# First products on half the tokens, one x tile normalized on ScalarE first, q/k weights ahead of the second x block, one tile transposed by matmuls

## The chip, the cores and the metric

One core of a Trainium2 chip. The metric is device time in microseconds (us) of one execution, lower is better. "Span" is the time from the first to the last instruction of the profiled execution; it is about 1.7 us shorter than that execution's device time. The engines: PE is TensorE, DVE is VectorE, ACT is ScalarE, POOL is GpSimd, SP is the queue that issues the transfers (SPq).

## The reference, cut to what matters

```python
def reference(A_x, A_wqkv, A_wo, B_x, B_w1, B_w3, B_w2):     # x: 1 x 2048 x 1024, bf16
    xn = _layernorm(x, axis=-1)          # (x - mean) / sqrt(var + 1e-5), over the 1024 columns
    s = _A_ref(xn, A_wqkv, A_wo)         # q, k, v = xn @ wqkv (1024 x 3072); local dilated attention; @ wo
    g = _silu(_B_ref(xn, B_w1, B_w3, B_w2))   # silu(xn @ w1) * (xn @ w3), then @ w2; F = 3584
    ...                                  # s and g are combined by a recurrence along the tokens (cut)
```

Only the first 40 us of the program are touched by the change: layer norm of the first 512 tokens (x block one, four tiles of 128 tokens), their transposition, the first products with wqkv, and the preparation of the second 512 tokens (x block two). The products are done by Strassen's scheme on blocks; "eq" and "bq" are the first accumulators that need sums of weights and *differences of x blocks one and two*.

## The kernel before: the parts that matter

```python
def spin(ps, n):                       # n matmuls of zeros, to keep TensorE warm
    for k in range(n):
        nc.tensor.matmul(ps[:, k % 2], lhsT=warm[:, 0:P], rhs=warm[:], start=True, stop=True)

def ln_dve(c, sts):                    # layer norm of x tiles on VectorE (root on ScalarE)
    ...
        for h in range(2):
            nc.vector.bn_stats(out=stats[:, h, :], in_=xt4[:, st, h * 512:(h + 1) * 512])
        nc.vector.bn_aggr(out=mv[:, i, :], in_=stats[:])
    nc.scalar.activation(out=rstd[:], in_=mv[:, :, 1], func=ACTF.Sqrt, bias=eps_t[:], scale=1.0)
    nc.vector.reciprocal(out=rstd[:], in_=rstd[:])
    ...                                # tensor_scalar: (x - mean) * rstd

def ln_act(c, sts):                    # the same on ScalarE: Copy and Square with sums, Sqrt, Identity
    ...                                # two small steps (reciprocal, product) on VectorE

def ln_tp(c, st, dst, busy=0):         # transposes one x tile by eight matmuls with the identity
    tp = bank2(f"tp{c}_{st}")
    spin(tp, busy)
    ...

def xn_sums(b11, b21, b12, b22, o):    # four differences of x blocks one and two, VectorE
    nc.vector.tensor_sub(o[:, 0], b12, b11)      # "eq" needs this one
    nc.vector.tensor_sub(o[:, 1], b22, o[:, 0])  # "bq" needs this one
    nc.vector.tensor_sub(o[:, 2], b22, b12)
    nc.vector.tensor_sub(o[:, 3], b21, o[:, 1])

x_load(0)                              # four x tiles
wq0 = qkv_load(0, 0, slot(2, (4, D)))  # 1 MB each
x_load(1)
wq1 = qkv_load(0, 1, slot(6, (4, D)))
for st in range(NST):
    (ln_act if st == 2 else ln_dve)(0, [st])
...
tps = [ln_tp(0, st, [], busy=(5, 0, 1, 1)[st]) for st in range(NST)]
...                                    # eight copies out of PSUM: tiles 0, 1 VectorE, tiles 2, 3 ScalarE
wk0 = qkv_load(1, 0, slot(8, (4, D)))
wk1 = ...
qkv_load(2, 0, wve[0][:])
for st in range(NST):
    ln_dve(1, [st])
    ...                                # two DMA transposes of the tile of x block two
    if st == 1:
        qkv_load(2, 1, wve[1][:])
x_load(2)
...
for t, (w0, w1_, ws) in enumerate(...):          # q, k, v
    first_two(...)                     # products of width 512 with x block one
qkv_sums(wq0, wq1, sq)
xn_sums(xT[:, 0], xT[:, 1], b12, xT[:, 2], xs)
```

The Python order is not the order on an engine: a scheduler orders the instructions, each engine then takes its own list strictly in that order. `hp()` (high priority) and `issue_after` steer it.

## Time and profile before

| | before |
|---|---|
| device time, median of the first 3 runs | 726.93 us (725.63 to 726.95) |
| device time, 6 runs beside the changed kernel | 726.22 us (725.63 to 726.95) |
| span of the profiled execution | 725.4 us |
| TensorE busy | 715.2 us |
| first product / first full-width product with wq1 | 12.23 / 16.09 us |
| "eq" / "bq" | 34.05 / 35.78 us |

The four landmarks are starts in TensorE's timeline. Behind "bq" TensorE runs nearly without waits to the end, except for one stall near 675 us.

### The profile page before, as it was taken

What the parts mean: (1) busy time and instruction counts of PE and PEld (TensorE: products, weight loads), DVE (VectorE), ACT (ScalarE), POOL (GpSimd) and SP (SyncE); (2) the same over time, 40 slices, a digit from 0 to 9 for tenths busy, and PEclk for the clock granted to TensorE, in tenths of its full rate; (3) what the DMA queues carried; (4) which work ended last, traced back from release to release, by engine and by line L of the source; (5) the groups of instructions that cost most, each with busy time, mean ns of one, the idle gap of its engine ahead of it and who ended that gap; (6) DMA issues with size and microseconds to landing.
All of it is one profiled execution on the core that took longest, in us unless ns stands there. A gap on an engine that the chain in (4) does not pass through costs nothing.

```text
span 725.4 us, 8725 instructions
## 1 busy us (share of the span) xinstructions
PE 715.2 (99%) x3335; PEld 344.1 (47%) x3335; DVE 622.8 (86%) x678; ACT 313.9 (43%) x325; POOL 111.7 (15%) x171
## 2 busy tenths in 40 slices
PE   8999999999999999999999999999999999999996
PEld 4655656554444444444444444444444444444442
DVE  8795879779879878978999999969859989978984
ACT  5654434356555556554545312034364573020233
POOL 0011100011310300332212010000434006020011
PEclk9999999999999999999999999999999999999999
DMA  9966156877755453566756556469799445564515
GB/s 325 278 155 171 59 188 215 266 237 255 225 176 180 145 174 116 178 189 199 248 166 229 184 160 219 144 203 379 175 282 321 144 136 160 167 195 140 188 27 111
DMA packets 120137, 139.77 MB, mean 193 GB/s; under 512 B 18592, under 2 KB 95392, under 8 KB 119456
## 3 DMA queue, kind: packets, MB, share of 16 engines
q1 hardware_dynamic: 105552, 97.27, 44.1%
q0 software_dynamic: 14544, 41.95, 18.8%
q8 instruction: 26, 0.43, 0.2%
q14 instruction: 15, 0.12, 0.1%
HBM read 96.21 MB, written 38.80 MB: 186 GB/s over the span
## 4 chain that ended last, share of the span: by engine, by line
PE 92%; DVE 3%; ACT 2%; DMA 1%; issue 1%; SPq 0%; DVEq 0%; ACTq 0%
PE bm L149 20%; PE am L149 13%; PE em L149 13%; PE db L149 10%; PE bq L149 9%; PE de L149 7%; PE da L149 7%; PE eq L149 5%; PE aq L149 3%; PE wb L149 2%; PE we L149 2%; PE wa L149 2%; DVE stats L250 1%; DMA wve<-in_A_wqkv_dram 1%; PE af L149 1%
## 5 line engine op out<-in xcount | busy, mean ns | idle before, releaser
L149 PEld LDWEIGHTS <-wring 128*128 128x128 f16 (+1 forms) x1824 | 187.9, 103 | 207.5 <-issue 1.9
L149 PEld LDWEIGHTS <-h_sb 128*128 128x128 f16 (+1 forms) x1056 | 109.6, 104 | 119.4 <-issue 2.0
L149 PE MATMUL bm<-xs,wring 128*128 128x512 f16 x504 | 117.4, 379 | 0.1
L149 PE MATMUL am<-xT,wring 128*128 128x512 bf16 x336 | 79.7, 379 | 0.1
L149 PE MATMUL db<-wring,h_sb 128*128 128x512 f16 x336 | 73.2, 379 | 0.0
L474 DVE TENSOR_TENSOR BC<-Ep,vT 128x2048 bf16<-128x2048 bf16 x56 | 66.7, 1219 | 0.1
L419 DVE TENSOR_TENSOR pt<-qt,kT 128x4096 bf16<-128x4096 bf16 x24 | 55.0, 2290 | 0.7
L657 DVE TENSOR_TENSOR um<-em,um 128x1024 f32<-128x1024 f32 x28 | 34.2, 1223 | 20.9 <-PE em L149 20.0
L659 ACT ACTIVATE g<-um 128x1024 bf16<-128x1024 f32 x28 | 29.6, 1057 | 48.2 <-DVE um L657 48.2
L149 PE MATMUL da<-wring,h_sb 128*128 128x512 bf16 x224 | 49.0, 379 | 0.0
L460 POOL DMA_DIRECT2D Ep<-pb x64 | 37.9, 599 | 53.7 <-DVE pb L456 46.6
L149 PE MATMUL bm<-h_sb,wring 128*128 128x512 f16 x168 | 39.7, 379 | 0.0
L149 PE MATMUL em<-xs,wring 128*128 128x512 f16 x168 | 39.7, 379 | 0.0
L149 PE MATMUL em<-xT,wring 128*128 128x512 bf16 x168 | 39.7, 379 | 0.0
L484 DVE TENSOR_TENSOR oT<-oT,BC 128x2048 bf16<-128x2048 bf16 x32 | 39.0, 1220 | 0.4
L159 ACT COPY bm<-am 128x1024 f32<-128x1024 f32 x28 | 27.9, 998 | 26.0 <-PE am L149 26.0
L159 ACT COPY pm<-em 128x1024 f32<-128x1024 f32 x28 | 28.4, 1013 | 20.1 <-PE em L149 20.1
L159 ACT COPY um<-bm 128x1024 f32<-128x1024 f32 x28 | 28.4, 1013 | 19.2 <-PE bm L149 19.2
L678 ACT CAST g<-bm 128x1024 bf16<-128x1024 f32 x28 | 28.3, 1010 | 17.4 <-PE bm L149 17.4
L672 DVE TENSOR_TENSOR h_sb<-bm,pm 128x1024 bf16<-128x1024 f32 x21 | 25.6, 1218 | 5.1 <-PE bm L149 5.0
L421 DVE TENSOR_TENSOR pt<-pt 128x2048 bf16<-128x2048 bf16 x24 | 29.3, 1222 | 0.4
L962 POOL DMA_DIRECT2D out_dram<-h_sb x12 | 15.1, 1512 | 94.7 <-DVE h_sb L961 94.6
(197 smaller groups left out, 1019.5 us busy)
## 6 DMA issues: line engine op xcount, KB each, us to landing
wring<-in_B_w_dram SPq DMA_DIRECT2D x61, 512.0 KB, 4.5
wring<-t_dram SPq DMA_DIRECT2D x16, 512.0 KB, 3.7
t_dram<-wring POOLq DMA_DIRECT2D x14, 512.0 KB, 4.6
wring<-t_dram SPq DMA_DIRECT2D x16, 384.0 KB, 5.1
wring<-in_B_w_dram SPq DMA_DIRECT2D x12, 384.0 KB, 4.0
wring<-in_A_x_dram SPq DMA_DIRECT2D x16, 256.0 KB, 4.7
Ep<-pb POOLq DMA_DIRECT2D x64, 64.0 KB, 4.6
wring<-in_A_wo_dram SPq DMA_DIRECT2D x8, 512.0 KB, 5.7
```

What stands on the lines that cost most here:

```text
L149: anchor["pe"] = nc.tensor.matmul(ps, lhsT=lhs[k], rhs=rhs[k], start=(first and k == 0), stop=(k == n - 1), skip_group_check=not first,)
L159: nc.scalar.copy(out=out_, in_=in_)
L419: nc.vector.tensor_mul(p_t[:], q[:], kT[:, :, o:o + CH])
L421: nc.vector.tensor_add(p_t[:, 0:4, :], p_t[:, 0:4, :], p_t[:, 4:8, :])
L460: nc.gpsimd.dma_start(out=pr[c][r:P:NR, :, sq * P:(sq + 1) * P], in_=pb[sq * 32:(sq + 1) * 32, :, :])
L474: nc.vector.tensor_mul(dst, E[:, w, :].unsqueeze(1).to_broadcast([P, n, CH]), vT[:, js, o:o + CH])
L484: nc.vector.tensor_add(A, A, B if w0 else C)
L657: v = nc.vector.tensor_add(su2[:], pe[:], su2[:])
L659: nc.scalar.activation(out=hl["g"][:, :, CH:], in_=su2[:], func=ACTF.Silu)
L672: anchor["v"] = nc.vector.tensor_add(h[:, :, CH:], pb[:], sp5[:])
L678: nc.scalar.copy(out=hl["g"][:, :, 0:CH], in_=pb[:])
L962: nc.gpsimd.dma_start(out=rows_, in_=g, accum_op=ALU.add)
```

## The change

Its intent: let TensorE begin real products sooner (on the first 256 tokens while the others are still transposed), have the weights there in the order of their use, and take the transfer queue out of the way of the second path (transposes of x block two, then the differences).

```diff
+    wq1 = qkv_load(0, 1, slot(6, (4, D)))
+    wk0 = qkv_load(1, 0, slot(8, (4, D)))
     x_load(1)
-    wq1 = qkv_load(0, 1, slot(6, (4, D)))
-    for st in range(NST):
-        (ln_act if st == 2 else ln_dve)(0, [st])
...
-    tps = [ln_tp(0, st, [], busy=(5, 0, 1, 1)[st]) for st in range(NST)]
...                      # tpose(st, a): four transposes; untp(st, a, engine): copy out of PSUM
+    ln_dve(0, [0])
+    ln_act(0, [1])
+    ln_dve(0, [2])
+    ln_dve(0, [3])
+    def p1(g, th):       # 8 matmuls of 256 columns: token half th, weight group g
+        cols = slice(th * 2 * P, (th + 1) * 2 * P)
...
+        act_copy(snap[g][:, :, cols], pf[g][:, :, cols])
+    spin_in(0, 0, 5)
+    tpose(0, 0)
+    tpose(0, 1)
+    untp(0, 0, dve_copy)
+    untp(0, 1, sc_copy)
+    tpose(1, 0)
+    tpose(1, 1)
+    untp(1, 0, sc_copy)
+    untp(1, 1, sc_copy)
+    tpose(2, 0)
+    tpose(2, 1)
+    untp(2, 0, dve_copy)
+    p1(0, 0)
+    tpose(3, 0)
+    tpose(3, 1)
...
+    p1(1, 0)
+    p1(0, 1)
+    p1(1, 1)
...
-    TPE = ()
-    qkv_load(2, 0, wve[0][:])
+    TPE = (3,)           # tile 3 of x block two is transposed by matmuls
+    for h in I:
+        qkv_load(2, h, wve[h][:])
...
-        if st == 1:
-            qkv_load(2, 1, wve[1][:])
...
-                  *((lambda: None, 4) if t == 0 else (lambda: None, 0)))
-    tp1(*TPE)
-    qkv_sums(wq0, wq1, sq)
+                  *((lambda: None, [pf[0], pf[1]]), (lambda: None,), (lambda: tp1(*TPE),))[t])
+    with behind("x"):
+        qkv_sums(wq0, wq1, sq)
```

Cut: the bookkeeping of `first_two`, which takes over the products already begun, and a priority for the square roots of x blocks one and two. Six of the warming matmuls, between the transposes and ahead of the first product, are gone.

More of the change, by code (lines that the diff above doesn't have):

```diff
@@ L165, in flush, with first_two @@
             pend.pop(0)()
-    def first_two(key, A, b11, b21, snap, e11, mid=lambda: None, busy=0):
-        pa = []
+    def first_two(key, A, b11, b21, snap, e11, mid=lambda: None, pa=None):
+        have, pa = pa, pa or []
         for g in range(2):
-            pa.append(bank2(f"a{key}{g}"))
-            spin(pa[g], busy if g == 0 else 0)
-            for i in I:
-                mm(pa[g][:, i], A[g][0][i], b11, True)
-            act_copy(snap[g], pa[g][:])
+            if have is None:
+                pa.append(bank2(f"a{key}{g}"))
+                for i in I:
+                    mm(pa[g][:, i], A[g][0][i], b11, True)
+                act_copy(snap[g], pa[g][:])
         mid()
@@ L251, in ln_dve @@
             nc.vector.bn_aggr(out=mv[:, i, :], in_=stats[:])
-        nc.scalar.activation(out=rstd[:], in_=mv[:, :, 1], func=ACTF.Sqrt, bias=eps_t[:], scale=1.0)
-        nc.vector.reciprocal(out=rstd[:], in_=rstd[:])
+        with hp() if c < 2 else nullcontext():
+            nc.scalar.activation(out=rstd[:], in_=mv[:, :, 1], func=ACTF.Sqrt, bias=eps_t[:], scale=1.0)
+            nc.vector.reciprocal(out=rstd[:], in_=rstd[:])
         for i, st in enumerate(sts):
@@ L297, in xn_sums @@
         nc.vector.tensor_sub(o[:, 2], b22, b12)
-        nc.vector.tensor_sub(o[:, 3], b21, o[:, 1])
+        anchor["xs"] = nc.vector.tensor_sub(o[:, 3], b21, o[:, 1])
     def B_of(b11, b21, b22, o):
@@ L986 @@
     qt[0] = att_tile((NJ, CH), BF16, "qt0")
-    tps = [ln_tp(0, st, [], busy=(5, 0, 1, 1)[st]) for st in range(NST)]
-    for a in I:
-        for st in range(NST):
-            (nc.vector.tensor_copy if st < 2 else nc.scalar.copy)(
-                out=xT[:, a, :, st * P:(st + 1) * P], in_=tps[st][:, a].rearrange("p (k t) -> p k t", k=KH),
-            )
-    wk0 = qkv_load(1, 0, slot(8, (4, D)))
+    snap = [oT[:, i // 2, 4 * (i % 2):4 * (i % 2) + 4].rearrange("p j n -> p (j n)").bitcast(FP32).rearrange("p (i n) -> p i n", i=2) for i in range(4)]
@@ new lines, with tpose, untp @@
+    tpb = {}
+    def tpose(st, a):
+        key = a, st // 2
+        if key not in tpb:
+            tpb[key] = bank2(f"tp{a}{st // 2}")
+        tp = tpb[key]
+        for k in range(KH):
+            nc.tensor.matmul(
+                tp[:, st % 2, k * P:(k + 1) * P], lhsT=xt[0][:, st, (a * KH + k) * P:(a * KH + k + 1) * P], rhs=ident[:],
+                start=(k == 0), stop=(k == KH - 1), skip_group_check=True,
+            )
+    def untp(st, a, eng):
+        with hp():
+            r = eng(out=xT[:, a, :, st * P:(st + 1) * P], in_=tpb[a, st // 2][:, st % 2].rearrange("p (k t) -> p k t", k=KH))
+        if eng == dve_copy:
+            anchor["x"] = r
@@ new lines @@
+    dve_copy, sc_copy = nc.vector.tensor_copy, nc.scalar.copy
+    ln_dve(0, [0])
+    ln_act(0, [1])
+    ln_dve(0, [2])
+    ln_dve(0, [3])
+    pf = {}
+    def p1(g, th):
+        if g not in pf:
+            pf[g] = bank2(f"af0{g}")
+        cols = slice(th * 2 * P, (th + 1) * 2 * P)
+        w = wq0.rearrange("p k (c two j) -> p k two j c", two=2, j=4)
+        for i in I:
+            for k in range(KH):
+                nc.tensor.matmul(
+                    pf[g][:, i, cols], lhsT=w[:, k, 0, 2 * g + i, :], rhs=xT[:, 0, k, cols],
+                    start=(k == 0 and th == 0), stop=(k == KH - 1), skip_group_check=True,
+                )
+        act_copy(snap[g][:, :, cols], pf[g][:, :, cols])
@@ new lines, in spin_in @@
+    def spin_in(st, a, n):
+        tpb[a, st // 2] = bank2(f"tp{a}{st // 2}")
+        spin(tpb[a, st // 2], n)
+    spin_in(0, 0, 5)
[13 more added lines that the diff above has]
+    tpose(3, 1)
+    untp(3, 0, dve_copy)
+    untp(2, 1, sc_copy)
+    untp(3, 1, dve_copy)
+    p1(1, 0)
@@ L1012 @@
     sq = [sq[:, q] for q in range(3)]
-    snap = [oT[:, i // 2, 4 * (i % 2):4 * (i % 2) + 4].rearrange("p j n -> p (j n)").bitcast(FP32).rearrange("p (i n) -> p i n", i=2) for i in range(4)]
     Bq = B0, B_of(xT1[0], xT1[1], xT1[3], xs1)
```

## The prediction

> **What bounds the kernel now.** I read the page first, then TensorE's own waits, then TensorE's timeline over the first 40 us, then the same stretch of the transfer queue and of VectorE, because the diff touches nothing after it.
>
> ```profile
> PE 715.2 (99%) x3335; PEld 344.1 (47%) x3335; DVE 622.8 (86%) x678; ACT 313.9 (43%) x325; POOL 111.7 (15%) x171
> ```
>
> TensorE is busy in 715.2 us of a span of 725.4 us. Only TensorE's idle time, or work of TensorE that is not needed, can be removed. Its waits are few:
>
> ```profile
> PE warm L141 <- DVE warm L138: 1.3, 1, 1.3
> PE de L149 <- ACT dsp L159: 1.1, 1, 1.1
> PE af L149 <- DMA wve<-in_A_wqkv_dram: 0.4, 1, 0.4
> PE af L149 <- DMA wring<-in_A_wqkv_dram: 0.2, 1, 0.2
> ```
>
> Two of these are in the stretch that is changed (both "af"), and they are small. But "busy" hides the head: until 12.23 us TensorE runs zero matmuls that keep it warm, and transposes. In TensorE's timeline the columns are start, busy time, instruction and, in brackets, the idle time before it:
>
> ```profile
> 7.89 1.35 PE L281 MATMUL tp<-ident,wring 128*128 128x128 bf16 x16 [0.36 <-DVE wring L255]
> 9.07 0.59 PE L141 MATMUL tp<-warm 128*128 128x512 bf16 x2
> 9.96 1.07 PE L281 MATMUL tp<-ident,wring 128*128 128x128 bf16 x16 [0.29 <-ACT wring L275]
> 11.13 1.04 PE L141 MATMUL af<-warm 128*128 128x512 bf16 x4
> 12.23 3.61 PE L149 MATMUL af<-xT,wring 128*128 128x512 bf16 x16
> 16.09 7.12 PE L149 MATMUL af<-xT,wring 128*128 128x512 bf16 x32 [0.24 <-DMA wring<-in_A_wqkv_dram]
> ...
> 26.50 3.62 PE L149 MATMUL af<-xT,wve 128*128 128x512 bf16 x16
> 30.54 3.67 PE L149 MATMUL af<-xT,wve 128*128 128x512 bf16 x16 [0.42 <-DMA wve<-in_A_wqkv_dram]
> 34.05 1.89 PE L149 MATMUL eq<-xs,h_sb 128*128 128x512 f16 x8
> 35.78 1.89 PE L149 MATMUL bq<-xs,h_sb 128*128 128x512 f16 x8
> ```
>
> From 12.23 us on the products follow each other at 16 per 3.46 us (23.05 to 26.50), 0.216 us each. Against that pace the second half of the first product lost 0.4 us (12.23 + 3.46 = 15.69, it begins at 16.09: the second q weight block landed at 16.04), and the last v half lost 0.58 us (26.50 + 3.46 = 29.96, begins at 30.54: the second v block was issued at 24.01, behind four transposes, and landed at 30.49). The remaining length of the program is TensorE at its pace, so what the head saves should arrive at the end almost whole. Every later stretch where VectorE waits (102 us in total) ties it to TensorE again; the last such wait for TensorE before the one 1.1 us stall (at 676.96) is at 583.5, so that stall moves along too.
>
> The second path is the one to watch. "eq" needs the first difference of the second x block, "bq" the third one that is made:
>
> ```profile
> 29.25 1.26 SPq L1004 DMA_TRANSPOSE xT<-wring  x1
> ...
> 31.95 1.23 DVE L295 TENSOR_TENSOR xs<-h_sb,xT 128x2048 f16<-128x2048 bf16 x1 [3.97 <-DMA h_sb<-wring]
> 33.09 1.22 DVE L297 TENSOR_TENSOR xs<-xT,h_sb 128x2048 f16<-128x2048 bf16 x1
> 34.23 1.22 DVE L296 TENSOR_TENSOR xs<-xT,xs 128x2048 f16<-128x2048 bf16 x1
> ```
>
> VectorE stood idle 3.97 us for the transposes, and its third difference is done at 34.23 + 1.22 = 35.45, only 0.33 us ahead of "bq" at 35.78. TensorE can come forward by little before this chain (transposes by DMA, then three differences) holds it.
>
> **What the Trainium skill says.** "TensorE: Matmul & The Clock Gate", section "Wait — 56ns, not 53.3ns?", gives warm starts of 55.6 ns apart at 128 columns and 215.7 ns at 512; the trace has 216 ns. My estimate for 256 columns from its formula, N / 2.4 GHz + 2.5 ns, is 109 ns, so halving the tokens of a product costs nothing in array time. The same page, "What's actually happening", has the clock halve after an idle window of about 3.4 us. The trace's first matmuls are 0.43 us apart up to 5.97 us and 0.21 us afterwards; the change drops six warming matmuls, and the longest gap that I expect in the new head is 1.5 us, so I expect full speed.
> "DMA: Bandwidth & Descriptors", "Queues, rings and completion order", says that descriptors of one engine's ring are consumed in order. The trace agrees: transfers land in the order of issue, 1 MB in 2.71 us (wq0 at 10.62, the x block at 13.33, wq1 at 16.04, wk0 at 18.75, wk1 at 21.46). That is 387 GB/s, above the 358 GB/s that "Where 436 GB/s comes from" on that page calls the HBM limit; the measurement decides.
>
> **The change part by part.** The instruction orders of the two programs differ on TensorE in the first ~310 entries, on VectorE in the first 85, on ScalarE in the first 33, on the transfer queue in the first dozen; behind that they are the same.
>
> 1. *Tile 1 normalized on ScalarE first, instead of tile 2.* Tile 1 lands at 4.12, tile 2 at 4.89. Copy 4.14 to 5.20, Square 5.5 to 6.6, Sqrt 7.0; VectorE's two small steps reach it at 8.2, Identity (1.24) ends at 9.45. Before, it ended at 9.90. Tile 3 on VectorE slips to 10.6 (before 9.28), which matters less now.
> 2. *First products on half the tokens.* ScalarE then does the square root of tile 3 (0.3) and two copies of 0.51: 10.8. The first 8 matmuls of 256 columns begin near 10.85 (wq0 lands at 10.62), take 8 x 0.109 = 0.87, to 11.7; tile 3's transposes 0.45 to 12.2; the second group to 13.1; the other halves of both groups 1.75, to 14.85, with VectorE's copy of tile 3 (0.62 after 12.0) and ScalarE's snapshots just ahead of them. The full-width products with wq1 then begin at 14.85, not 16.09: **1.24 us gained**, if wq1 is there, and it now lands third, at 10.62 + 2.71 = 13.33.
> 3. *Weights ahead of x block two.* wk0 at 16.04, x tiles at 16.7 to 18.75, wk1 21.46 as before, v blocks 24.1 and 26.9 (no longer split by transposes). TensorE needs wk0 at 18.3, wk1 at 21.75, v at 25.2 and 29.2: no wait. **0.58 us gained** at the v block.
> 4. *One tile by matmuls:* 8 x 0.056 = **0.45 to 0.5 us added** on TensorE between the two v halves, and two ScalarE copies of 0.51; two of eight DMA transposes go (1.25 us of issue each).
>
> Sum on TensorE's own path: 1.24 + 0.58 - 0.5 = 1.3 us; "eq" at 32.7, "bq" at 34.45.
>
> The other path: VectorE now makes the q sums first (3 x 1.14, from 13.6 to 17.0), then the statistics of x block two; tile 0 is normalized near 20.8 (before 15.2), tiles 1 and 2 near 23.5 and 24.0. The transposes so begin 5.5 us later and queue behind the second v block (26.85). From the trace's pattern (the fourth was issued just as the block ahead landed, later ones every 1.25 us, landing 1.8 us after issue), the fifth lands near 30.4 and the sixth near 31.7. VectorE's k sums end near 30.4, ScalarE's copies of the tile by matmul near 31.0. Three differences from 30.5, the second waiting for the last transpose: 31.7, 32.9, 34.05. "bq" may begin at 34.1 against TensorE's 34.45. Both paths give the same gain within their error: **about 1.3 us**, 726.9 - 1.3 = 725.6.
>
> **The rivals.** (a) The transposes become the bound: if their issue takes 2.5 us each, as the first two of before did, the sixth lands near 33.8, the differences end near 36.1, and all is lost: 727. For it: they are later by 5.5 us and behind 2 MB more; against it: two fewer, nothing between them, and the long issues fell while the queue was full. (b) ScalarE's serial work (its statistics, four copies and four snapshots between 4 and 15 us) delays the halves, or wq0 lands after 10.9: gain under 0.5 us, 726.5. (c) The clock falls in the sparser head: up to 2 us of half speed, 727. (d) More is won: the copies overlap better and wq1's early arrival takes all the slack: 2 us, 724.9.
>
> **Range and chances.** The before runs alone spread from 725.63 to 726.95. I take 725.5, from 724.2 to 727.0. Two per cent are 14.5 us; before the first product there are only 12.2 us, so neither faster nor slower by over 2% is likely.
>
> **What would show it.** First product near 10.9 with 256 columns; full-width products from 14.9 without a wait for wq1; no wait for the v block; "bq" near 34.4. If a wait of TensorE for VectorE's differences stands at "eq" or "bq", rival (a) has happened. Matmuls of 256 columns 213 ns apart would show (c). The prediction is wrong if the gain at "bq" is not there at the end, or if it is above 2.5 us.

## More of the kernel before

The prediction shows TensorE's lines. What it does not show, and what became important, is VectorE's timeline of the kernel before (columns: start, busy time, instruction, count, and in brackets the idle time before it with what ended it):

```profile
3.52 1.88 DVE L250 BATCH_NORM_STATS2 stats<-wring 128x6 f32<-128x512 bf16 x3 [2.28 <-DMA wring<-in_A_x_dram]
...
5.43 1.23 DVE L250 BATCH_NORM_STATS2 stats<-wring 128x6 f32<-128x512 bf16 x2
6.58 0.14 DVE L253 RECIPROCAL rstd<-rstd 128x1 f32<-128x1 f32 x1
...
7.30 0.53 DVE L255 TENSOR_SCALAR wring<-wring,mv,rstd 128x1024 bf16<-128x1024 bf16 x1
```

Tile 0 landed at 3.50 and its statistics take two instructions, but its scaling stands at 7.30, behind the statistics of other tiles. If one of those lands late, tile 0 waits as well. In this profile none was late enough to show a wait.

## The result

| | before | after |
|---|---|---|
| device time, 6 runs each | 726.22 us (725.63 to 726.95) | 725.22 us (724.67 to 727.57) |
| ratio after / before | | 0.999 (95% interval 0.9975 to 1.0005) |
| span of the profiled execution | 725.4 | 723.5 |
| first product | 12.23 | 10.88 |
| first full-width product with wq1 | 16.09 | 14.83 |
| first product with wk1 (af<-xT,h_sb) | 23.05 | 21.74 |
| "eq" / "bq" | 34.05 / 35.78 | 32.64 / 34.37 |
| stall near 675 us | 1.09 | 0.56 |

Ratios are the mean time of one kernel's fast runs over that of the other's of the same rounds, so not quite the ratio of the medians quoted. The result is correct. 725.5 was predicted, 725.22 came out.

TensorE's timeline of the changed kernel, from its first product to "bq" (columns as before). The counts of the groups can be too small: some matmul records are missing from the trace (the page counts 3299 matmuls against 3353 weight loads), so starts are read here, not counts:

```profile
10.88 1.03 PE L1022 MATMUL af<-xT,wring 128*128 128x256 bf16 x8
...
12.20 2.79 PE L1022 MATMUL af<-xT,wring 128*128 128x256 bf16 x24
14.83 7.07 PE L149 MATMUL af<-xT,wring 128*128 128x512 bf16 x31
...
25.28 3.62 PE L149 MATMUL af<-xT,wve 128*128 128x512 bf16 x15
28.73 0.61 PE L282 MATMUL tp<-ident,wring 128*128 128x128 bf16 x8
29.18 3.62 PE L149 MATMUL af<-xT,wve 128*128 128x512 bf16 x16
32.64 1.89 PE L149 MATMUL eq<-xs,h_sb 128*128 128x512 f16 x8
34.37 1.89 PE L149 MATMUL bq<-xs,h_sb 128*128 128x512 f16 x8
```

No bracket stands behind any of these: from its first product up to "bq" TensorE waits for nothing. Half products follow at 24 in 2.63 us (12.20 to 14.83), 0.110 us each, half of the 0.216 us of a full one. The three largest waits of TensorE (engine and line, what it waited for, us in total, times, longest):

```profile
PE warm L141 <- DVE warm L138: 1.3, 1, 1.3
PE de L149 <- ACT dsp L159: 0.6, 1, 0.6
PE tp L997 <- DVE wring L256: 0.5, 1, 0.5
```

Both waits for weights are gone; the third line and two smaller ones lie ahead of the first product. The second path, VectorE's differences:

```profile
30.47 1.23 DVE L296 TENSOR_TENSOR xs<-h_sb,xT 128x2048 f16<-128x2048 bf16 x1 [0.32 <-ACT h_sb L288]
31.61 1.22 DVE L298 TENSOR_TENSOR xs<-xT,h_sb 128x2048 f16<-128x2048 bf16 x1
32.75 1.22 DVE L297 TENSOR_TENSOR xs<-xT,xs 128x2048 f16<-128x2048 bf16 x1
```

What "bq" needs is done at 32.75 + 1.22 = 33.97, 0.40 us ahead of "bq"; it was 0.33 us before. Its last wait is no more for a DMA (3.97 us before) but 0.32 us for ScalarE's copy of the tile that matmuls transposed.

"bq" is 1.41 us earlier, and the same 1.41 us stands at the landmarks behind it ("zp" 155.29 to 153.88 and 482.41 to 481.00). The span is 1.83 us shorter, since the stall near 675 us is also 0.53 us smaller (1.41 + 0.53 = 1.94; 0.1 us is lost elsewhere). So the trace says 1.4 us, the medians say 1.0 us, and the interval of the ratio includes zero. Two questions follow: does each part of the change do what its working says, and why do the runs of one kernel spread more (724.67 to 727.57) than the gain?

### The profile page after: what moved, and what is told of

The parts are those of the page before. It is cut to its first block, busy times and chain, and to the rows that moved or that the text cites. A ratio compares the mean times of both kernels' runs of the same rounds, so it can differ in the third digit from the quotient of the medians.

```text
span 723.5 us, 8711 instructions
## 1 busy us (share of the span) xinstructions
PE 711.4 (98%) x3299; PEld 345.8 (48%) x3353; DVE 623.2 (86%) x678; ACT 314.8 (44%) x329; POOL 111.9 (15%) x171
## 4 chain that ended last, share of the span: by engine, by line
PE 80%; DVE 7%; issue 6%; ACT 2%; DMA 2%; POOL 2%; DVEq 0%; ACTq 0%; POOLq 0%
PE bm L149 18%; PE am L149 13%; PE em L149 12%; PE bq L149 9%; PE eq L149 5%; PE db L149 5%; PE de L149 4%; PE da L149 3%; PE aq L149 3%; PE af L149 2%; PE wb L149 2%; DVE BC L475 2%; PE we L149 1%; PE wa L149 1%; POOL Ep L461 1%
## 5 line engine op out<-in xcount | busy, mean ns | idle before, releaser
L149 PEld LDWEIGHTS <-wring 128*128 128x128 f16 (+1 forms) x1808 | 185.7, 103 | 205.4 <-issue 1.6
```

The lines of the kernel that those rows point to most:

```text
L149: anchor["pe"] = nc.tensor.matmul(ps, lhsT=lhs[k], rhs=rhs[k], start=(first and k == 0), stop=(k == n - 1), skip_group_check=not first,)
```

## The experiments

**Theory.** The parts act as in the prediction's sum, TensorE's own path sets "bq", and the path of transposes and differences is 0.4 us behind it. **Rivals.** The head is set by something the sum takes as fixed (when x tiles land, in which order VectorE works); or the clock of TensorE falls in some executions; or the second path takes over as soon as a part is changed.

All twelve kernels give correct results. Profiles, landmarks in us from the span's start; "tile 2" is the landing of x tile 2 of block one, "full" the first full-width product with wq1:

| run | tile 2 | first | full | eq | bq | stall | span |
|---|---|---|---|---|---|---|---|
| before | 4.89 | 12.23 | 16.09 | 34.05 | 35.78 | 1.09 | 725.4 |
| after | 5.16 | 10.88 | 14.83 | 32.64 | 34.37 | 0.56 | 723.5 |
| e1 again | 5.84 | 11.57 | 15.52 | 33.34 | 35.06 | 0.26 | 723.9 |
| e2 full width | 5.78 | 12.76 | 16.25 | 34.31 | 36.67 | none | 725.5 |
| e3 all by DMA | 5.29 | 11.02 | 14.96 | 32.94 | 35.45 | 0.30 | 724.2 |
| e4 v split | 5.88 | 11.61 | 17.20 | 37.14 | 38.87 | none | 727.5 |
| e5 x first | 5.49 | 11.23 | 15.59 | 33.34 | 35.07 | 0.34 | 724.0 |
| e6 tile 2 on ScalarE | 5.46 | 11.49 | 15.44 | 33.25 | 34.98 | 0.56 | 724.2 |
| e7 steps on GpSimd | 5.63 | 11.78 | 16.72 | 34.44 | 36.17 | 0.90 | 725.7 |
| e8 e7 + order of differences | 6.01 | 11.81 | 15.55 | 33.27 | 35.00 | 0.58 | 724.2 |
| e9 warming matmuls | 5.83 | 11.78 | 15.66 | 33.52 | 35.25 | none | 723.8 |
| e10 order of VectorE | 5.29 | 11.32 | 15.32 | 33.04 | 34.77 | 0.87 | 724.3 |
| e11 several together | 5.86 | 10.90 | 17.85 | 35.88 | 37.60 | none | 726.1 |
| e12 before, again | 5.66 | 15.13 | 18.58 | 35.85 | 37.58 | 0.95 | 727.0 |

Span minus "bq" minus stall is 688.5 to 688.8 us in every row. So the profiled span is "bq", plus that constant, plus the stall: the stall is a second source of spread, and it does not follow "bq" (none at 35.25 and at 37.60, 1.09 at 35.78 and 0.95 at 37.58). The traces settle what sets it. In every profile GpSimd issues a load, vT<-v_dram, 613.2 us behind "bq" (613.5 in e2), VectorE waits for it, and the chain of VectorE's work that ends the stall starts there. VectorE's timeline of the kernel before:

```profile
654.66 1.22 DVE L474 TENSOR_TENSOR oT<-Ep,vT 128x2048 bf16<-128x2048 bf16 x1 [6.03 <-DMA vT<-v_dram]
```

The load lands 4.43 to 5.62 us after its issue, and in all ten profiles with a stall the stall is that time less 4.53 us, to 0.01 us (5.62 and 1.09 before, 5.08 and 0.56 after, 4.79 and 0.26 in e1). In the four without one it took 4.43 to 4.53. So the 0.53 us that the stall gave the changed kernel's profile are the chance of one transfer, not a gain of the change.

### e1: the changed kernel, unaltered

No edit.

> The changed kernel, unaltered, as a control. Main theory: the gain is made in the head of TensorE's timeline and only shifts the rest, so a second profile has the first product at 10.9 us, full-width products from 14.8, bq at 34.4, and in the timed rounds about 1.0 us (0.14%) less than before. The stall of TensorE near 675 us, which was 1.1 us in the profile of before and 0.6 us in that of after, is chance: anywhere from 0.4 to 1.2 here. Rival: that stall was shortened by the change and is 0.6 again.

725.67 us (725.15 to 726.09, 5 runs) against 726.15 for before; ratio 0.9994 (0.9981 to 1.0006). In its profile the head is 0.69 us later at every landmark. VectorE's timeline of this run:

```profile
5.87 0.69 DVE L250 BATCH_NORM_STATS2 stats<-wring 128x6 f32<-128x512 bf16 x1 [0.71 <-DMA wring<-in_A_x_dram]
6.48 0.15 DVE L254 RECIPROCAL rstd<-rstd 128x1 f32<-128x1 f32 x1
```

Tile 0's reciprocal stands behind the first statistics of tile 2, and these wait 0.71 us for tile 2, which landed at 5.84 instead of 5.16. First product minus landing of tile 2 is 5.72 (after), 5.73 (e1, e3, e4) and 5.74 (e5) in the five profiles with this head: the landing passes through one for one. The prediction's sum takes this landing as fixed. So the expectation failed: the landmarks came 0.7 us late, the gain was about 0.5 us by the medians and not 1.0, and the stall of 0.26 us lies below the 0.4 to 1.2 expected. That the stall is chance, and not an effect of the change as the rival has it, is borne out by the load described above.

### e2: halving undone

```diff
-        cols = slice(th * 2 * P, (th + 1) * 2 * P)
+        cols = slice(0, CH)
...                      # p1(0, 0) and p1(1, 0) only, after all the transposes
```

> Halving undone: the first products wait for all four tiles, everything else as in the changed kernel. Main theory: first product near 12.1 us (tile 3 normalized at 10.8, transposed to 11.3, copied by VectorE to 12.0), full-width second half 16 x 0.216 later at 15.55 instead of 14.83, no wait for a weight block, bq at 35.1, time 0.7 us longer than the changed kernel, so about 0.3 us under before. Rival (the halves are not what gains; the other path sets bq anyway): bq within 0.2 us of 34.4 and the same time.

727.21 us (726.87 to 728.20), ratio to before 1.0017; 1.54 us above e1's median of the same rounds. Against e1, whose tile 2 landed nearly alike: first product +1.19, full width +0.73, as expected; but "bq" +1.61, twice what was expected. VectorE's timeline shows the rest:

```profile
32.44 0.69 DVE L250 BATCH_NORM_STATS2 stats<-wring 128x6 f32<-128x512 bf16 x1 [2.68 <-DMA wring<-in_A_x_dram]
33.05 1.21 DVE L296 TENSOR_TENSOR xs<-h_sb,xT 128x2048 f16<-128x2048 bf16 x1
```

The scheduler put a statistics instruction of x block *three* ahead of the first difference, and VectorE stood 2.68 us until its data landed, though the first difference had its last input at 31.76; TensorE waited 0.19 us at "eq" and 0.44 us at "bq". So halving is worth 0.73 us at the full-width products, confirmed, and the other 0.9 us belong to an order that changed with the edit.

### e3: no tile by matmuls

```diff
-    TPE = (3,)
+    TPE = ()
```

> All four tiles of x block two transposed by DMA, as before; no matmul transposes there; everything else changed. Main theory: the two added transposes land near 31.6 and 32.9 us, so the three differences end near 35.2 and TensorE, which would be ready for bq at 33.9, begins it near 35.2: about 0.9 us lost against the changed kernel, with waits of TensorE for VectorE at eq and bq. Rival (the matmul transposes only cost TensorE 0.45 us and hide nothing): bq near 33.9 and a time 0.45 us shorter.

726.74 us (725.91 to 727.47), ratio 1.0008; 1.07 us above e1's median of the same rounds. TensorE's timeline:

```profile
32.94 1.92 PE L149 MATMUL eq<-xs,h_sb 128*128 128x512 f16 x8 [0.46 <-DVE xs L296]
35.45 1.89 PE L149 MATMUL bq<-xs,h_sb 128*128 128x512 f16 x8 [0.59 <-DVE xs L297]
```

The last two transposes landed at 31.46 and 32.75 (31.6 and 32.9 expected), and TensorE waits for the differences twice. In the changed kernel "bq" is 34.37 - 14.83 = 19.54 us behind the first full-width product, without a wait; counted from 14.96, "bq" would stand at 34.50 with the tile by matmuls, and at 34.06 without it if nothing waited (the tile takes 0.44 us, shown below). It stands at 35.45. So the tile costs 0.44 us of TensorE and saves 1.39 us of delay, 0.95 us net; 0.9 was expected. Here the second path sets "bq": the rival is real at a distance of one transposed tile.

### e4: the second v block behind four transposes, as before

```diff
-    for h in I:
-        qkv_load(2, h, wve[h][:])
+    qkv_load(2, 0, wve[0][:])
...
+        if st == 1:
+            qkv_load(2, 1, wve[1][:])
```

> The second v block issued behind the transposes of two tiles, as before; everything else changed. Main theory: it is issued near 26.4 us and lands near 29.9, TensorE needs it at 29.18 and waits 0.6 to 0.9 us; eq near 33.4, bq near 35.2; time 0.7 us longer than the changed kernel. Rival (the wait for the v block was covered by the differences in any case): bq within 0.2 us of 34.4 and the same time.

730.09 us (729.22 to 732.23), ratio 1.0065, the slowest of all. Two causes, in TensorE's timeline:

```profile
11.61 1.53 PE L1022 MATMUL af<-xT,wring 128*128 128x256 bf16 x8
...
33.63 3.67 PE L149 MATMUL af<-xT,wve 128*128 128x512 bf16 x16 [2.00 <-DMA wve<-in_A_wqkv_dram]
```

First, the v block was issued at 27.75 and landed at 33.58, 4.64 us after the fourth transpose (28.94). In the kernel before it landed 2.88 us after that transpose (27.61 and 30.49), and a block behind another block there took 2.64 to 2.71 us. TensorE waited 2.00 us, where 0.6 to 0.9 was expected. The block lost its time at its start: the core's transfers ran at 78 GB/s from 29 to 30 us, 207 from 30 to 31 and 410 from 31 to 32. In the kernel before it was issued 3.60 us ahead of the fourth transpose's landing, here 1.19 us; that this is the reason is not shown. Second, eight half products took 1.53 us instead of 1.03 in the same head: TensorE's clock fell. Between first and full-width product lie 5.59 us, not 3.95, so 1.64 us were lost. That has nothing to do with the edit, which comes 16 us later; all four timed runs of e4 have a mean granted clock of 0.993 to 0.996. Hence the rival of the falling clock, told below. With two causes mixed, the time of e4 is no measure of the v block's order; the wait of 2.00 us is, for this one execution.

### e5: x block two ahead of wq1 and wk0

```diff
+    x_load(1)
     wq1 = qkv_load(0, 1, slot(6, (4, D)))
     wk0 = qkv_load(1, 0, slot(8, (4, D)))
-    x_load(1)
```

> Order of loads undone: x block two ahead of the second q block and the first k block; everything else changed. Main theory: the second q block lands near 15.2 us instead of 12.5, TensorE, ready at 14.83, waits about 0.4 us; k and v blocks land in time; differences not later; bq near 34.8, time 0.4 us longer than the changed kernel. Rival (early x tiles matter more, because VectorE's statistics and the transposes start earlier): bq at or under 34.4 and the same or a shorter time.

726.12 us (725.42 to 727.41), ratio 0.9995. wq1 landed at 15.52; TensorE would have been ready at 11.23 + 3.95 = 15.18 and began at 15.59, 0.41 us late. That is the size expected, but the wait expected is not the one in the trace. TensorE's timeline:

```profile
13.79 1.97 PE L1022 MATMUL af<-xT,wring 128*128 128x256 bf16 x16 [0.20 <-DVE xT L1004]
```

The eight half products ahead of these began at 12.54, so at 0.110 us each the next were due at 13.42; they began at 13.79, 0.37 us late, because VectorE's copies of tile 3 came behind statistics of x block two, which had landed earlier in this order. The last of these sixteen began at 15.49 and the full-width product 0.11 us after it, so wq1, there since 15.52, cost nothing more. Alone it would have cost about 0.4 us: two delays lie over each other. The new order of loads is worth about 0.4 us here, but the run does not show which of the two it removes.

### e6: tile 2 on ScalarE instead of tile 1

```diff
-    ln_act(0, [1])
-    ln_dve(0, [2])
+    ln_dve(0, [1])
+    ln_act(0, [2])
```

> Tile 2 on ScalarE and tile 1 on VectorE, as before; everything else changed. Main theory: tile 1 is normalized by VectorE near 8.3 us, but its copies out of PSUM stay on ScalarE, which is busy with tile 2 until about 9.95, so the first product begins near 11.0 and the full-width products near 15.0; time 0.2 us longer than the changed kernel. Rival (tile 1 on ScalarE is what makes the early start): first product later than 11.5 and 0.6 us or more lost.

726.10 us (725.69 to 728.52), ratio 1.0003. TensorE waits 1.56 us for ScalarE's tile and begins its products at 11.49; with tile 1 on ScalarE and the same landing (5.46) it would be 5.46 + 5.73 = 11.19. The choice of the tile is worth 0.3 us.

### e7 and e8: tile 1's small steps on GpSimd; the order of the differences

```diff
...                      # mhalf: a constant tile of -0.5
-        nc.scalar.activation(out=v[:, 2], in_=v[:, 1], func=ACTF.Sqrt, bias=eps_t[:], scale=1.0 / D)
...
-            nc.vector.reciprocal(out=v[:, 2], in_=v[:, 2])
-            nc.vector.tensor_mul(v[:, 3], v[:, 0], v[:, 2])
+            nc.gpsimd.tensor_scalar(out=v[:, 2], in0=v[:, 1], scalar1=1.0 / D, scalar2=1e-5, op0=ALU.mult, op1=ALU.add)
+            nc.gpsimd.tensor_tensor(out=v[:, 2], in0=v[:, 2], in1=mhalf[:], op=ALU.pow)
+            nc.gpsimd.tensor_mul(v[:, 3], v[:, 0], v[:, 2])
```

> A step beyond the change: tile 1's reciprocal square root and product are made on GpSimd (three tiny instructions) instead of Sqrt on ScalarE and two steps behind statistics on VectorE; ScalarE then need not wait 1.03 us (7.4 to 8.46) before Identity. Main theory: Identity starts near 7.7, first product near 10.1 (the first q block lands at 9.8 to 10.6), full-width products near 14.1; a wait of 0.1 to 0.2 for the second k block; TensorE ready for bq at 33.7 but the three differences end at 33.97, so bq near 34.0: 0.3 to 0.4 us gained of 0.7. Rival (TensorE's path alone counts): bq at 33.7.

e8 adds to that an order: what "bq" needs is made second of the four differences.

```diff
+        o1 = nc.vector.tensor_sub(o[:, 1], b22, o[:, 0])
+        with tc.issue_after(o1.ins):
+            nc.vector.tensor_sub(o[:, 2], b22, b12)
```

> As the previous one, and the difference that bq needs is made second instead of third (it ends 1.1 us earlier). Main theory: bq at 33.7, that is 0.7 us before the changed kernel's 34.4, and a time about 0.7 us under it, 1.7 under before. Rival: no further gain over the previous one.

e7: 726.53 us (725.39 to 727.39), ratio 0.9998. e8: 726.03 us (725.36 to 727.44), ratio 0.9997. The attempt failed: ScalarE's Identity of tile 1 began at 8.90 in e7, not at 7.7 (GpSimd's three instructions, begun at 6.91, 7.80 and 8.68, stood among others of its own list), so nothing came earlier, and e8 could not show its gain because the head never put the second path to the test ("bq" has no wait in it, at 35.00). But e7's profile shows the clock. TensorE's work by stretch of 3 us (columns: stretch, length, busy time and count of PE, PE weight loads, DVE, ACT, POOL, then the granted clock, the DMA share and GB/s), e7:

```profile
8.00:11.00 3.00, 1.30 (x17) 0.89 (x15) 2.96 (x9) 2.10 (x4) 1.01 (x5) 0.98 1.04 395
11.00:14.00 3.00, 3.00 (x21) 2.40 (x20) 1.02 (x2) 1.13 (x3) 0.00 (x0) 0.50 1.05 393
```

The clock is at half for these 3 us although TensorE is busy throughout them; the stretch ahead is the one with little work. Half products stand 213 to 214 ns apart there. The prediction named exactly this as the sign of its rival (c).

### e9: warming matmuls put back

```diff
+    spin_in(2, 0, 3)     # three, between tile 0's transposes and the next
...
+            spin(pf[g], 1 if g == 0 else 0)
```

> The changed kernel with three 512-column warming matmuls between tile 0's transposes and the next ones, and one ahead of the first product; nothing else altered. Theory: some executions of the changed kernel let TensorE's clock fall to half in the head, because six warming matmuls of the kernel before are gone and the gaps lie closer together; with the gaps filled, no execution has a granted clock of 0.997 or lower, none lies near 727.5 us, the fastest and the median stay where the unaltered kernel has them (725.2 to 725.7, within 0.3), because the warming matmuls stand in time in which TensorE waits anyway (0.52 us idle after tile 0). First product 10.88 + (landing of x tile 2 - 5.16) as before, within 0.2. Rival: the low clock and the outliers come from elsewhere; then some of the executions still show 0.993 to 0.997. Second rival: the warming matmuls delay the products; then first product is 0.3 to 0.6 us later and so is the time.

725.35 us (724.85 to 725.50, 5 runs), ratio 0.9988 (0.9975 to 1.0000). Every run has a clock of 0.998 or more and none is an outlier; the first product is 5.95 us after tile 2's landing, 0.22 us later than without (0.2 was the bound expected). That is otherwise what the theory expected, but the timed runs do not settle it: five clean runs also came from the unaltered e1. The trace says more, below.

### e10: VectorE's order

```diff
-                nc.vector.bn_stats(out=stats[:, h, :], in_=xt4[:, st, h * 512:(h + 1) * 512])
+                with behind("s" if (c, st) == (0, 2) and h == 0 else "m" if c == 0 and st >= 2 else "xs" if c == 2 else None):
+                    nc.vector.bn_stats(out=stats[:, h, :], in_=xt4[:, st, h * 512:(h + 1) * 512])
...                      # "s": tile 0's scaling, "m": tile 1's small steps, "xs": the fourth difference
```

> The changed kernel with VectorE's queue in another order: tile 0's reciprocal and scaling ahead of the statistics of tile 2, tile 1's two small steps ahead of the second half of tile 2's statistics, and the statistics of x block three held behind the four differences. Theory: in the changed kernel the first product follows the landing of x tile 2 one for one, since the statistics of tile 2 stand ahead of tile 0's reciprocal in VectorE's strict order; with them behind it, the first product begins at 10.4 to 10.9 us whatever tile 2 does up to a landing of 6.2 us (unless wq0 lands later than that), full-width products near 14.7, bq near 34.3, and VectorE shows no wait for a DMA between 5 and 8 us. Rival: the landing acts through something else (tile 3, ScalarE, the weights); then the first product stays at about 5.7 us after tile 2's landing (10.88 for 5.16, 11.57 for 5.84).

725.29 us (725.07 to 725.95, 4 runs), ratio 0.9987 (0.9972 to 1.0002). Half confirmed. VectorE no longer waits for a DMA after 3.62, and ScalarE's Identity of tile 1 begins at 7.47 instead of 8.46. But the first product came at 11.32, outside the 10.4 to 10.9 expected, and even 0.3 us later than the rival's 5.29 + 5.73 = 11.02. TensorE's timeline:

```profile
9.59 0.73 PE L998 MATMUL tp<-ident,wring 128*128 128x128 bf16 x8 [1.24 <-ACT xT L1005]
10.60 0.62 PE L998 MATMUL tp<-ident,wring 128*128 128x128 bf16 x8 [0.27 <-DVE wring L257]
```

Tile 1 was ready at 8.71, but its transposes waited until 9.59 for ScalarE's copy of tile 0. In the changed kernel tiles 0 and 1 share one tile "tp" in PSUM (where TensorE's results stand until they are copied out), and the program lets tile 1 be written into it only after tile 0 has been copied out; that copy stands behind the Identity on ScalarE. In the kernel before each tile had its own. One wait was removed, and the next one took its place.

### e11: several together, meant to beat both

```diff
...                      # e10's order, e8's order of the differences, and:
+    spin_in(2, 0, 4)
+    with behind("spin"):
+        tpose(1, 0)
...
+    with behind("t11"):
+        p1(0, 0)         # first products ahead of the transposes of tiles 2 and 3
+    with behind(("p", 0, 0)):
+        tpose(2, 0)
+        tpose(2, 1)
...
```

> A version meant to beat both: e10's order of VectorE, tile 1's first copy directly after tile 0's on ScalarE, the first eight products ahead of the transposes of tiles 2 and 3, four warming matmuls between tile 0's and tile 1's transposes, and bq's difference second of the four (e8). Theory: first product at about 10.1 to 10.3 us, or at wq0's landing if that is later (9.3 to 10.6 in the runs so far), full-width products at 14.0 to 14.5, eq near 32.0 to 32.3, bq 33.7 to 34.0, no granted clock of 0.997 or lower; time 0.5 to 1.0 us below the unaltered changed kernel, about 724.8. Rival (wait replaced): eq or bq waits for VectorE's differences, the first of which ended at 31.6 in the changed kernel; then bq stays at 34.3 or later and the time is that of the changed kernel, 725.2 to 725.7. A difference below 0.5 us can be told only roughly, since the stall at 675 us has varied from 0.26 to 1.09 by chance.

727.82 us (726.42 to 728.21, 5 runs), ratio 1.0020 (1.0006 to 1.0033): slower than both, neither theory nor rival. TensorE's timeline and its stretches:

```profile
9.85 0.61 PE L1001 MATMUL tp<-ident,wring 128*128 128x128 bf16 x8 [2.02 <-DVE xT L1008]
10.90 1.86 PE L1024 MATMUL af<-xT,wring 128*128 128x256 bf16 x8 [0.45 <-ACT xT L1008]
```

```profile
8.00:11.00 3.00, 0.70 (x9) 0.72 (x10) 2.45 (x7) 2.12 (x6) 0.00 (x0) 0.99 1.05 391
11.00:14.00 3.00, 3.00 (x21) 2.65 (x21) 1.40 (x3) 1.11 (x3) 0.00 (x0) 0.50 1.06 398
```

The same shared PSUM tile: tile 1's transposes waited 2.02 us for VectorE's copy of tile 0, which my order had put behind the statistics of tile 3. Tile 0 and the warming matmuls were over sooner, so the gap is longer than any other in the changed family, and the clock fell: eight half products in 1.86 us. Four of five runs have a clock of 0.995 or 0.996 (the fifth, 726.42, has 0.998).

### e12: the kernel before, unaltered

> The kernel before, unaltered, for a second profile. Theory: its head varies too (the order of VectorE's queue is the scheduler's there as well), so the first profile's 12.23 / 16.09 / 34.05 / 35.78 is one draw, and the stall near 677 us (1.09 there, 0.26 to 1.09 in the changed kernel) is another; expected: first product within 0.7 of 12.23, bq within 0.7 of 35.78, stall between 0.2 and 1.1. Rival: the kernel before is fixed by the landing of its weights and stays within 0.15 us at every landmark; then the gain of the change varies only by the changed kernel's own head.

728.73 us, one run, while nine timed runs of the same kernel in the same rounds gave 725.26 to 727.49. The theory's direction was right and its size far too small: the first product came 2.90 us later than in the first profile, "bq" 1.80 us later. VectorE's timeline, then TensorE's:

```profile
8.19 0.69 DVE L250 BATCH_NORM_STATS2 stats<-wring 128x6 f32<-128x512 bf16 x1 [2.09 <-DMA wring<-in_A_x_dram]
```

```profile
10.11 1.52 PE L281 MATMUL tp<-ident,wring 128*128 128x128 bf16 x16 [3.50 <-DVE wring L255]
```

x tile 3 landed at 8.16 instead of 5.90. Its statistics stand ahead of tile 0's reciprocal in the kernel before, so TensorE had nothing for 3.50 us, and then ran at half clock from 11.1 to 14.6 us. Of the 2.90 us, 1.10 disappeared again up to "bq": the waits of 0.24 and 0.42 us for weights that the first profile shows are not there, since a later TensorE finds its weights landed.

### The clock, over all profiles

Busy time of TensorE from 8 to 11 us, and the granted clock from 11 to 14 us:

| clock from 11 to 14 us | runs: TensorE busy in 8 to 11 us |
|---|---|
| 1.00 | before 2.60, after 1.93, e8 1.76, e5 1.71, e9 1.55, e10 1.49, e3 1.40, e1 1.35, e2 1.30, e6 1.25 |
| 0.67 | e4 1.39 (0.77 from 14 to 17 us) |
| 0.50 to 0.52 | e7 1.30, e12 0.79, e11 0.70 |

All drops follow a stretch with under half of its time busy, but not all such stretches bring a drop: e1 and e4 have the same head to 0.04 us, one keeps its clock and one does not. The Trainium skill, "TensorE: Matmul & The Clock Gate", section "What's actually happening", says that the clock is set by the activity of a window of 3413 ns that is free-running. The traces agree. Their clock records (in each trace.npz; a record is a start, a length and a share of the clock) put whole windows between two changes: in e4, e7, e11 and e12 full clock for 6827 ns, half for 3413, then full again; in all fourteen the last stretch of full clock is 208 to 210 windows long. So each profile's windows can be laid out from its first record of full clock, and TensorE's work in them counted. The window that holds most of the transposes, in e4 and then in e1 (columns as in e7):

```profile
8.58:12.00 3.42, 1.79 (x20) 1.43 (x21) 2.90 (x8) 2.82 (x5) 0.00 (x0) 1.00 1.05 405
9.13:12.54 3.41, 2.37 (x26) 1.99 (x27) 2.32 (x6) 2.95 (x5) 0.00 (x0) 1.00 1.02 387
```

The same head is cut 0.55 us apart. e4's window has 1.79 us of work, and half clock follows at 12.00; e1's has 2.37, and the clock stays. In all fourteen profiles, from that record on, half clock follows every window with 1.79 us of work or less (0.93 in e12, 0.94 in e11, 1.66 in e7, 1.79 in e4, and those at the program's end) and no window with 1.87 (e8) or more. So the phase of the window decides between equal heads, and the limit lies near 1.8 us of 3.41 in these traces (roughly: some matmul records are missing). It also shows what e9's warming matmuls are worth: its window from 8.26 to 11.67 holds 1.96 us of work; in e1, whose tile 2 landed 0.01 us later, the same stretch holds 1.57. With that phase the unaltered kernel would have lost its clock (an estimate from these two traces).

In the timed runs a mean granted clock of 0.997 or less occurs in 1 of 27 runs of the kernel before in the experiments' rounds, in 2 of 6 of the changed kernel and 0 of 5 of e1. In the trace of e4 a drop costs 1.64 us. The changed kernel's outlier at 727.57 had 0.997, but so had its fastest run at 724.67: the mean over a whole span shows a drop of 3 us too weakly to charge single runs with it. e10's profiled run has 0.997 as well, and its head kept the full clock.

## Why the prediction was right

The number is within 0.3 us, and its mechanism held in each term that the two profiles can show. The closeness owes something to luck. The sum starts from a median of three runs, 726.93; six runs put it at 726.22, from which the same 1.3 us lead to 724.9. And in the changed kernel's profile tile 2 landed at 5.16, just when VectorE was done with tile 0 (5.17): in e1, e3 and e5, with the same head, it landed later and the first product with it, at 11.57, 11.02 and 11.23. The terms:

- *TensorE's own path sets the end.* The 1.41 us gained at "bq" arrives whole at every later landmark, and span = "bq" + 688.5 to 688.8 + stall holds in fourteen profiles.
- *First product near 10.85, full width at 14.85, "eq" 32.7, "bq" 34.45.* Measured 10.88, 14.83, 32.64 and 34.37. e2 confirms the worth of the halving (0.73 us at the full-width products), e5 the size of that of the order of loads (0.41 us; the wait for wq1 that the term names is hidden there by another delay), e6 that of the tile on ScalarE (0.3 us).
- *0.58 us at the v block.* The wait is gone; e4, which puts it back, loses 2.00 us by it. So the term is right for the schedule of the kernel before; that the undivided order is worth more in the changed one rests on this one execution.
- *0.45 to 0.5 us for the tile by matmuls.* The two v halves begin 29.18 - 25.28 = 3.90 us apart; 3.46 are products, so 0.44 us. e3 shows that the tile pays: without it "bq" is 0.95 us later.
- *The other path allows "bq" at 34.1.* Measured 33.97. The fifth and sixth transposes landed at 29.02 and 30.24, not at 30.4 and 31.7, because they were issued earlier; ScalarE's copies of the matmul tile (expected near 31.0) were done at 30.43 and 30.93, and the first of them was then the last input of the first difference to arrive. Two errors of 1.4 us in the transposes cost nothing, since it was not they that ended the wait.
- *Rival (a), transposes as the bound,* did not happen but stands 0.40 us away; e3 makes it happen. *Rival (b)* did not happen. *Rival (c)*, the falling clock, did not happen in the profiles of the changed kernel, but in e4, e7 and e11, whose heads are like it; its timed runs do not show whether it did. *Rival (d)* did not happen: nothing was won beyond the sum at "bq" but 0.1 us, and the 0.53 us of the stall are chance.

Wrong was a reason, not the number: the prediction expects full speed because the longest gap would be 1.5 us, as if the length of one gap decided. In e7 the longest gap between 7 and 11 us was 1.33 us and the clock fell; in e9 it was 1.45 us and it did not; the work in the clock's window decided. It also reads the stall as tied to TensorE, so that it "moves along": the load behind it does (613.2 us behind "bq"), but its landing varies by more than 1 us. Nor is the last wait of VectorE for TensorE ahead of the stall at 583.5: one stands at 607.71, and the wait for that load at 654.66. (Its list of TensorE's waits leaves out two of six, 0.36 and 0.29 us, which stand in its next view; the sum does not rest on them.) And the prediction treats the head as one schedule: it took tile 2's landing as given, where the same kernel's first product followed it from 10.88 to 11.57, half of the whole gain. The same dependence on a late tile, in a worse form, is in the kernel before (e12). This, with the stall and the clock, is why a gain of 1.4 us in one pair of profiles is 1.0 us by the medians of the same rounds and 0.5 us in e1's.

What stays open: what delays a transfer by 1 to 2 us in one execution and not in another (an x tile at the start, the load ahead of the stall); why the v block of e4 was slow to start; how often the clock falls in the changed kernel.

## What to carry to other kernels

Look for what stands *ahead* of the first useful instruction in each engine's strict order: a statistics instruction of a later tile in front of tile 0's reciprocal handed every delay of that later tile to the first product, one for one. When a wait is removed, ask what the freed instruction will meet next (here a shared PSUM tile) before the versions are combined. And where an improvement is smaller than the spread of the starting stretch, take the landmarks of several profiles, not one pair, and check the granted clock of the stretch, not the mean of the span.

## What the Trainium skill lacked or had wrong

- "TensorE: Matmul & The Clock Gate", "What's actually happening": its table has the clock at half "after ≥1 idle window (~3.4µs)". In e7 it fell after a window with 1.66 us of work and no gap above 1.33 us, in e4 after 1.79 us of work. A window without work is not needed. How much work a window must have is not stated; here 1.79 us of 3.41 lost the clock and 1.87 us kept it.
- "DMA: Bandwidth & Descriptors", "Where 436 GB/s comes from": it says that the HBM side (about 358 GB/s) binds transfers from HBM, and does not say there that this is the share of a core when two stream, as the same page does under "Measured (HBM→SBUF, 128 partitions, SWDGE, issued from GpSimd)". With one core running, weight blocks of 1 MB landed every 2.71 us, 387 GB/s.
- No page that I read says what a plain transfer costs between DMA transposes in the same queue: a block of 1 MB landed 2.88 us after the transpose ahead of it in the kernel before, 2.86 in e12 and 4.64 in e4; directly behind another block it took 2.53 to 3.69 us in the fourteen profiles.
- No page that I read says how much the landing of one and the same transfer varies between executions: x tile 2 landed at 4.89 to 6.01 us and x tile 3 at 5.90 to 8.16 us in fourteen profiles, each issued at the same time to 0.01 us; the load ahead of the stall took 4.43 to 5.62 us.
